# A fused attention and expert kernel: half-wide second-level products, paced transfers, and nine routing operations on GpSimd

## The chip, the cores and the metric

The kernel runs on one core of one Trainium2 chip. The time is device time in microseconds (us) of one launch, as the median of several runs. Engines are called as in the profile: PE is TensorE's matrix multiply, PEld its weight load, DVE is VectorE, ACT is ScalarE, POOL is GpSimd and SP is SyncE, which here only issues transfers.

## The reference: what is computed

```python
# attention: q, k, v of (8 batches, 8 heads, 576, 64), tau = 0.02
scores = np.matmul(q, k.transpose(0, 1, 3, 2)) / 8
thresh = np.max(scores, axis=-1, keepdims=True) - tau
scores = np.where(scores >= thresh, scores, -1e9)
attn = np.exp(scores - np.max(scores, axis=-1, keepdims=True))
attn = attn / (np.sum(attn, axis=-1, keepdims=True) + 1e-09)
x = np.matmul(attn, v).transpose(0, 2, 1, 3).reshape(4608, 512)
# experts: token_ids (4608,), w1 (8, 512, 1024), w2 (8, 1024, 512)
expert_idx = token_ids * 2654435761 % 8
for e in range(8):
    mask = expert_idx == e
    out[mask] = np.maximum(x[mask] @ w1[e], 0.0) @ w2[e]
```

Everything is fp32. Each of the 4608 rows of x goes through one expert, so about 576 rows fall to each.

## The kernel before, in words

**Attention (0 to about 466 us).** The work is cut into 32 pairs of heads, numbered p; head pair hp = p // 8 and batch b = p % 8. A pair has five steps: s = 0 takes the 64 last queries of both heads, s = 1 to 4 take 128 queries each. The main loop (L710 on) counts n = 5p + s up to LAST = 160 and a few steps more, and is written as one hand-made order of instructions, which the engines follow. In a step PE forms scores for the step after it (`score`, L235), DVE negates them with a running minimum (`negate`, L246), ACT takes the exponential (`expo`, L260), POOL computes the threshold (thr, L253), DVE masks (`mask`, L271), PE transposes the weights of the step before the last (L282), ACT copies them to SBUF (`put_wT`, L303), and PE multiplies them with v (L313). At s = 1 POOL adds the epsilon to the sums (`add_eps`, L343) and scales the next pair's keys (`scale_k`, L215); at s = 2 DVE takes the reciprocal (L740). At s = 0 of the pair after the next, DVE multiplies by it into the tile xm (`put_xm`, L352), and SP stores xm to x_scratch in DRAM, about 3.6 us until it has landed.

**Routing, beside attention.** `route()` is a Python generator whose pieces are put into the main loop at s = 3 and s = 0 (for p = 9, 11, 13 also at s = 2). It turns token ids into expert numbers, counts places per expert with a table of ones (`onehot`, 8 x 36 columns) and a running sum (`incl`), orders the experts by their row count (`key`, `pos`, `order`), and gives each token a slot (`base`, `rank`, `slot_i`). `scatters()` (L536 on) then writes the token numbers to their slots by 36 indirect transfers of POOL (L542), one at the end of a step except at s = 1, in pairs 13 to 21. `fetch_early` (L119, through `gather`) gathers 15 of the 20 column blocks of the first expert's x rows, head pairs 0 to 2, at the start of a step with s = 0 and at the end of one with s = 3 or 4, in pairs 26 to 31; the last five gathers follow attention.

**Experts (about 476 to 918 us).** Experts are worked on in order of their row count: e = 0 has 544 columns of rows, e = 1 to 4 have 576, e = 5 to 7 have 600 (layer 2 of e = 7: 480 and a remainder of 120, `last_tile`). Layer 1 is w1 (512 x 1024) in two groups of 256 + 256 output rows, layer 2 is w2 (1024 x 512). Layer 1 of e = 0 is done plainly (`early_h`, L640, and `late_h`, L658 to L666, which adds the last head pair's part). All others go through `seven`: a 2x2 block product with seven products of half-size blocks in place of eight (Strassen's scheme in Winograd's form: sums s1 to s4 of the left blocks, t1 to t4 of the right ones). Each product is 8 matmuls of 128 x 128 weights and of half the expert's columns (in layer 1, 4 in each of the two groups). DVE forms the sums of blocks (L858) and, from each product in PSUM, the running sums u2, u3, u4 and the outputs (L861), ACT copies the first product (p1, L951) and takes the relu (L948). The products take turns between two pairs of PSUM tiles (`bank2`).

Beside them, hung into the products as `side` work: DVE turns the next expert's gathered rows by 32x32 squares (`turn_x`, L1064) and SP moves them into xT; POOL gathers the rows of the expert after it (`fetch`); SP loads its weights; DVE transposes the outputs oT by squares (`put_squares`, L1033), and POOL sends each square of 32 rows to the output (L1042), with two copies of `stok_odd` after each as a pause (L1027).

Of the kernel before, what the change touches and what calls it, by code (L numbers as in the profile page):

```python
# [9 lines left out]
FP32 = mybir.dt.float32  # L10
# [10 lines left out]
def kernel(  # L21
# [122 lines left out]
    with tc.tile_pool(name="a_q", bufs=1) as a_q, \  # L144
# [221 lines left out]
        def route():  # L366
# [38 lines left out]
            nc.vector.tensor_copy(eidf[:], eid[:])  # L405
            yield
            yield
            nc.vector.tensor_tensor(out=onehot[:],
                                    in0=eidf[:, None, :].to_broadcast([P, E, NTC]),
                                    in1=iota_f[:, 0:E, None].to_broadcast([P, E, NTC]),  # L410
                                    op=ALU.is_equal)
            yield
            for e in (0, E // 2):
# [6 lines left out]
                if e == 0:  # L420
                    yield
            yield
            nc.vector.tensor_copy(row[:], incl[:, :, NTC - 1])
# [13 lines left out]
            nc.vector.scalar_tensor_tensor(out=key[:], in0=cnt[:, E:2 * E], scalar=float(E),  # L437
                                           in1=iota_f[:, 0:E], op0=ALU.mult, op1=ALU.add)
# [10 lines left out]
            for e0, d in STEPS:  # L449
# [15 lines left out]
            nc.vector.tensor_copy(ot[:], ot_i[:])  # L465
# [3 lines left out]
            nc.vector.tensor_tensor(out=base[:], in0=oend[:], in1=ot[:], op=ALU.subtract)  # L469
# [3 lines left out]
            nc.vector.scalar_tensor_tensor(out=base[:], in0=base[:], scalar=8192.0,  # L473
                                           in1=cnt[:, 0:E], op0=ALU.mult, op1=ALU.add)
            nc.gpsimd.tensor_tensor(out=base[:], in0=base[:], in1=pos[:], op=ALU.add)
            yield
            nc.vector.tensor_tensor(out=incl[:], in0=incl[:],
# [3 lines left out]
            nc.vector.tensor_tensor(out=incl[:], in0=incl[:], in1=onehot[:], op=ALU.mult)  # L481
# [189 lines left out]
        G0 = NS * ((HP - 1) * B + 2)  # L671
# [16 lines left out]
        with tc.manual_schedule():  # L688
# [21 lines left out]
            for n in range(LAST + NS + 1):  # L710
                p, s = divmod(n, NS)
                m = n - 2
                if s == 0:
                    fetch_early(n)
# [85 lines left out]
                if s != 1 and placed:  # L800
                    next(scatter_pieces, None)
                if s > 2:
                    fetch_early(n)
# [23 lines left out]
    with tc.tile_pool(name="m_x", bufs=1) as m_x, \  # L827
         tc.tile_pool(name="m_o", bufs=3) as m_o, \
# [9 lines left out]
        o_end = m_x.tile([P, DIN], FP32, name="o_end")  # L838
# [4 lines left out]
        w2_s = m_s.tile([P, 3, FH, D2], FP32, name="w2_s")  # L843
        h_s = m_s.tile([P, 3, FH, CH], FP32, name="h_s")
        halves = [m_s.tile([P, 2, CH], FP32, name=n) for n in ("p1", "u2", "u3", "u4")]
# [3 lines left out]
        turn = [0]  # L849

        def bank2():
            turn[0] ^= 1
            if turn[0]:
                return ps_sc.tile([P, 2, 512], FP32, name="sc")
            return ps_m.tile([P, 2, 512], FP32, name="bank2")
# [31 lines left out]
        def w2_sums(e):  # L887
            t = triple(w2_s, 0, FH)
            return t if e == E - 1 else [dealt(x, C2) for x in t]
# [19 lines left out]
        def sums_w2(e):  # L909
            s1 = None  # L910
            if e == E - 1:
                spare = w_pool.tile([P, CO, F], FP32, name="w1_sb")
                s1 = w_tiles["s1"] = spare[:, :, 0:D2]
            return left(*w2_blocks(e, w_tiles[e, 2]), w2_sums(e), s1)
# [11 lines left out]
        def seven(a, a_s, b, b_s, m0, outs, relu, after):  # L926

            (a11, a12, s1, a22), (s2, s3, s4) = a, a_s
            (b11, t1, b21, b22), (t2, t3, t4) = b, b_s
            c11, c12, c21, c22 = outs  # L930
            n_k, width, dealt_out = a11.shape[1], b11.shape[2], len(a11.shape) == 4
            p1, u2, u3, u4 = (t[:, :, 0:width] for t in halves)

            def product(x, y):
                ps = bank2()
                for i in range(2):
                    c0 = m0 + P * i
                    for c in range(n_k):
                        lhsT = (x[:, c, :, i] if dealt_out else
                                x[:, c, c0:c0 + P])  # L940
                        nc.tensor.matmul(ps[:, i, 0:width], lhsT=lhsT, rhs=y[:, c],  # L941
                                         start=c == 0, stop=c == n_k - 1)
                return ps[:, :, 0:width]

            def out(c, ps, u, step):
                add(c, ps, u)()
                if relu:
                    nc.scalar.activation(c, c, AF.Relu)  # L948
                after(step)

            nc.scalar.copy(p1, product(a11, b11))  # L951
            out(c11, product(a12, b21), p1, 0)
            add(u2, product(s2, t2), p1)()
            after(1)
            add(u3, product(s3, t3), u2)()
            after(2)
            out(c21, product(a22, t4), u3, 3)
            k5 = product(s1, t1)
            add(u4, k5, u2)()
            out(c22, k5, u3, 4)  # L960
            out(c12, product(s4, b22), u4, 5)

        def layer1(e, side):

            w, half = w_tiles.pop((e, 1)), caps[e] // 2
            for g in range(NG):
                outs = [h_0[:, FH * i + 2 * g:FH * i + 2 * g + 2, half * k:half * k + half]
                        for i in range(2) for k in range(2)]
                seven(w1_blocks(w), triple(w1_s, 0, C2), x_blocks(e), triple(x_s, 0, C2, half), 2 * P * g,
                      outs, True, lambda step: side(g, step))  # L970

        def layer2(e, side):
# [5 lines left out]
            if e == E - 1:  # L978
                a[2] = w_tiles["s1"]
            seven(a, w2_sums(e), h_blocks(0, FH, half),  # L980
                  triple(h_s, 0, FH, half), 0, outs, False, side)

        def last_tile(middle):

            w, o_sb, idx = w_tiles[E - 1, 2], o_end, gidx[:, KT - 1:KT]
# [11 lines left out]
        def put_out(e, *groups):  # L997
# [14 lines left out]
            for tr, kts in zip(trs, groups):  # L1012
                for i, kt in enumerate(kts):
                    rows = rows_of(kt)
                    o_sb = m_o.tile([P, DIN], FP32, name="o_sb")
# [8 lines left out]
        def pause():  # L1024

            for _ in range(2):
                nc.gpsimd.tensor_copy(stok_odd[:], stok[:])  # L1027
# [49 lines left out]
        with tc.manual_schedule():  # L1077
            run(sums_w2(0), 4)
            fill(18)
            late_h(lambda fo: (ps_sc.tile([P, 2, 512], FP32, name="sc") if fo in (2, 4) else  # L1080
                               ps_m.tile([P, 2, 512], FP32, name="bank2")))
            fetch(1)
            run(sums_h(0, 0, FH), 4)

        with tc.manual_schedule():
            for e in range(E):
# [3 lines left out]
                if e > 0:  # L1090
                    w2_work, h_work = sums_w2(e), sums_h(e, 0, 2)

                    def side1(g, step):
                        if g == 0:
                            run(w2_work)
                            if step == 0:
                                put_squares(e - 1, 1)
                        else:
                            run(h_work)
                        if step > 2:  # L1100
                            run(turns, 1 if g == 0 else 2)
# [3 lines left out]
                x_work = (sums_w1(e + 1) + sums_x(e + 1)) if more else []  # L1105

                def side2(step):
                    if step == 0:
                        run(turns, len(turns))
                    else:  # L1110
                        run(x_work, 2)
# [4 lines left out]
                    if more and step == 3:  # L1116
# [24 lines left out]
        with tc.For_i(0, n_ov, 1) as it:  # L1141
# [26 lines left out]
            o_sb = m_o.tile([P, DIN], FP32, name="o_sb")  # L1168
# [36 lines left out]
```

## Time and profile before

| what | value |
|---|---|
| median of 3 runs | 925.46 us (924.17 to 926.12) |
| the profiled execution | 926.27 us |
| its span, first to last instruction | 924.6 us |
| granted TensorE clock | 0.999 |
| PE / DVE / ACT / POOL busy | 906.9 / 759.9 / 457.3 / 550.1 us |
| attention's loop | 0 to about 466 us |
| experts' stage | about 476 to 918 us |
| last PE record ends | 917.7 us |

The profile is of one execution, 1.67 us longer than its span. A group of instructions shows the line, engine, operation, output and inputs with their shapes, the count, the busy time in us and the mean of one in ns, then the idle time before them. "[0.28 <-issue]" in the order of time means that the engine was idle for 0.28 us before the instruction and that no releaser is seen in the records. A wait is put down to the event that came last. Matmuls are pipelined, so their records overlap: two records' starts tell the rate, not their lengths.

### The profile page before, as it was taken

The page shows a single profiled execution, that of the slowest core. Times are in us where ns is not written, and L with a number is a line of the kernel's source. Part 1 is how long each engine was busy: PE and PEld are TensorE (multiplying, and loading weights), DVE is VectorE, ACT ScalarE, POOL GpSimd, SP SyncE. Part 2 cuts the span into 40 slices and gives each one's busy share as a digit, 9 for nine tenths or more (in the row PEclk, how much of TensorE's full clock was granted, in tenths as well). Part 3 has the DMA queues.
Part 4 walks back from the last instruction along what each step waited for, and adds up shares of the span by engine and source line. Part 5 has one row for each costly group of instructions (what it writes and reads, how often), then busy time and mean ns, then how long its engine had stood idle before and what let it go on. Part 6 is the DMA issues. An engine that isn't in the chain of part 4 may idle for free.

```text
span 924.6 us, 21039 instructions
## 1 busy us (share of the span) xinstructions
PE 906.9 (98%) x7495; PEld 661.6 (72%) x7495; DVE 759.9 (82%) x1654; ACT 457.3 (49%) x741; POOL 550.1 (59%) x842
## 2 busy tenths in 40 slices
PE   7999999999999999999999999999999999999997
PEld 4666666656666666565668879788887978879785
DVE  8999999999999999999945696867768685786741
ACT  6888888888888898788922020110202011020210
POOL 4233432456666623446414588787787877878773
PEclk9999999999999999999999999999999999999999
DMA  7454463554545668734011636445252543522001
GB/s 175 95 146 123 107 152 96 134 134 101 124 100 149 167 164 220 209 96 108 16 33 56 195 118 185 136 125 196 63 199 90 170 155 90 218 61 67 28 28 62
DMA packets 114777, 113.13 MB, mean 122 GB/s; under 512 B 32475, under 2 KB 89315, under 8 KB 114672
## 3 DMA queue, kind: packets, MB, share of 16 engines
q1 hardware_dynamic: 105168, 92.64, 37.0%
q0 software_dynamic: 9072, 18.91, 6.6%
q8 instruction: 61, 1.00, 0.4%
q14 instruction: 44, 0.36, 0.1%
q10 hardware_dynamic: 432, 0.21, 0.1%
HBM read 81.99 MB, written 21.44 MB: 112 GB/s over the span
## 4 chain that ended last, share of the span: by engine, by line
PE 83%; POOL 6%; issue 4%; DVE 3%; ACT 2%; DMA 1%; SPq 0%; POOLq 0%; DVEq 0%; ACTq 0%
PE bank L941 18%; PE av L313 18%; PE sc L941 18%; PE sc L235 14%; PE tr L282 11%; POOL out_dram L1042 4%; PE sc L640 3%; POOL stok_odd L1027 2%; PE av L282 1%; DVE ns L246 1%; DVE w L271 1%; ACT w L260 1%; DMA k_sb<-in_k_dram 1%; ACT wT_b L303 1%; PE bank L658 0%
## 5 line engine op out<-in xcount | busy, mean ns | idle before, releaser
L260 ACT ACTIVATE w<-ns,nmx 128x576 f32<-128x576 f32 x288 | 220.4, 776 | 28.6 <-DVE ns L246 27.9
L271 DVE SCALAR_TENSOR_TENSOR w<-ns,thr,w 128x576 f32<-128x576 f32 x288 | 225.7, 816 | 0.0
L253 POOL TENSOR_SCALAR thr<-nmx,drop 128x2 f32<-128x2 f32 (+1 forms) x160 | 104.4, 652 | 188.9 <-DVE ns L246 179.1
L246 DVE TENSOR_SCALAR_CACHE_REDUCE ns<-sc 128x576 f32<-128x576 f32 x288 | 205.7, 746 | 8.5 <-PE sc L235 7.7
L235 PE MATMUL sc<-k_sb,q 64*128 64x288 f32 (+1 forms) x1280 | 178.2, 422 | 1.1 <-DVE ns L246 0.6
L282 PEld LDWEIGHTS tr<-ident,w 64*128 64x128 f32 x2624 | 105.6, 138 | 96.9 <-ACT wT_b L303 35.3
L1042 POOL DMA_INDIRECT out_dram<-o_q,qidx x127 | 139.7, 1100 | 57.8 <-issue 49.2
L282 PE MATMUL tr<-ident,w 64*128 64x64 f32 x2624 | 139.2, 230 | 7.7 <-ACT wT_b L303 4.8
L1027 POOL COPY stok_odd<-stok 128x152 int32<-128x152 int32 x314 | 139.9, 445 | 10.0
L948 ACT ACTIVATE h<-h 128x576 f32<-128x576 f32 (+1 forms) x56 | 38.8, 693 | 142.8 <-DVE h L861 142.0
L235 PEld LDWEIGHTS sc<-k_sb,q 64*128 64x128 f32 (+1 forms) x1280 | 92.2, 177 | 23.5 <-DVE ns L246 9.8
L313 PE MATMUL av<-wT_a,v 128*64 128x320 f32 (+1 forms) x704 | 100.4, 418 | 0.2
L303 ACT COPY wT_a<-tr 128x512 f32<-128x512 f32 (+1 forms) x128 | 81.7, 638 | 20.6 <-PE tr L282 20.1
L303 ACT COPY wT_b<-tr 128x512 f32<-128x512 f32 (+1 forms) x128 | 81.3, 635 | 18.2 <-PE tr L282 10.2
L313 PE MATMUL av<-wT_b,v 128*64 128x256 f32 x640 | 83.2, 389 | 0.0
L313 PEld LDWEIGHTS av<-wT_a,v 128*64 128x64 f32 x704 | 43.7, 136 | 29.0 <-DVE xm L352 0.7
L951 ACT COPY p<-bank 128x576 f32<-128x576 f32 (+2 forms) x11 | 7.0, 634 | 107.5 <-PE bank L941 102.5
L313 PEld LDWEIGHTS av<-wT_b,v 128*64 128x64 f32 x640 | 40.2, 136 | 18.8 <-issue 0.7
L119 POOL DMA_INDIRECT xg<-x_scratch,gidx_x x35 | 41.8, 1193 | 19.2 <-issue 9.3
L542 POOL DMA_INDIRECT slot_scratch<-tok,slot_i x36 | 44.9, 1247 | 9.5 <-issue 7.6
L951 ACT COPY p<-sc 128x576 f32<-128x576 f32 (+2 forms) x11 | 7.0, 637 | 84.7 <-PE sc L941 79.8
L941 PE MATMUL bank<-h,w_sb 128*128 128x288 f32 (+3 forms) x192 | 48.1, 404 | 0.0
(198 smaller groups left out, 1402.4 us busy)
## 6 DMA issues: line engine op xcount, KB each, us to landing
w_sb<-in_moe_w_dram SPq DMA_DIRECT2D x16, 2048.0 KB
q<-in_q_dram SPq DMA_DIRECT2D x62, 288.0 KB
v<-in_v_dram SPq DMA_DIRECT2D x32, 256.0 KB
x_scratch<-xm SPq DMA_DIRECT2D x32, 256.0 KB
xT<-xq SPq DMA_DIRECT2D x84, 80.0 KB
k_sb<-in_k_dram SPq DMA_DIRECT2D x31, 144.0 KB
k_sb<-in_k_dram SPq DMA_DIRECT2D x32, 112.0 KB
x_scratch<-xg SPq DMA_DIRECT2D x9, 256.0 KB
```

Of the source, the lines that this page charges most:

```text
L235: nc.tensor.matmul(sc[out_rows, i, 0:S2], lhsT=q_sb[rows, h, q0:q1], rhs=k_sb[rows, h], start=True, stop=True)
L246: nc.vector.tensor_scalar(out=ns[:].rearrange("p (i s) -> p i s", i=2), in0=sc[:, :, 0:S2], scalar1=-1.0, scalar2=None, op0=ALU.mult, op1= ...
L253: nc.gpsimd.tensor_scalar(out=thr[:, 0:j + 1], in0=stats[n][0][:, 0:j + 1], scalar1=drop[:], scalar2=None, op0=ALU.add)
L260: nc.scalar.activation(w, nss[n, j][:], AF.Exp, bias=stats[n][0][:, j:j + 1], scale=-1.0)
L271: nc.vector.scalar_tensor_tensor(out=w, in0=nss.pop((n, j))[:], scalar=stats[n][1][:, j:j + 1], in1=w, op0=ALU.is_le, op1=ALU.mult, accum_ ...
L282: nc.tensor.transpose(dst[:, r, 64 * c:64 * c + 64], src[rows, c0:c0 + P], ident[rows, rows])
L303: nc.scalar.copy(dst, tr[:, :, 0:64 * n_c].rearrange("p r (c q) -> p r c q", c=n_c))
L313: nc.tensor.matmul(av[64 * j:64 * j + 64, g, c0:c1], lhsT=v_sb[:, c, 64 * j:64 * j + 64], rhs=wT[g][:, i, c0:c1], start=(c == 0), stop=stop)
L542: nc.gpsimd.indirect_dma_start(out=slot_dram[c % 2][:, :], out_offset=bass.IndirectOffsetOnAxis(ap=slot_i[:, c:c + 1], axis=0), in_=tok[:, ...
L941: nc.tensor.matmul(ps[:, i, 0:width], lhsT=lhsT, rhs=y[:, c], start=c == 0, stop=c == n_k - 1)
L1027: nc.gpsimd.tensor_copy(stok_odd[:], stok[:])
L1042: inst = nc.gpsimd.indirect_dma_start(out=rows[:, :], out_offset=bass.IndirectOffsetOnAxis(ap=idx, axis=0), in_=o_sb, in_offset=None, boun ...
```

## The change

Three things are changed.

1. **Routing.** Nine of the operations in `route()` go from DVE to POOL: the copies to eidf, row and ot, the one-hot table (one operation with two broadcast inputs becomes eight comparisons with a constant), the key (one operation becomes two), the two steps of base (the second becomes two), and the two large operations on incl. Their places between the yields stay nearly the same.
2. **Transfers.** Scatters stand at the end of steps s = 0 to 3 in place of 0, 2, 3 and 4. Early gathers begin one pair earlier and stand at the end of steps 2 and 3, and of step 4 only for n < 135; none stands at the start of s = 0. The last is at s = 2 of the last pair (n = 157).
3. **Experts.** `seven` is split into a class `Seven` whose methods can be interleaved, and whose products go on accumulating in a PSUM tile (start=False) in place of additions by DVE; ACT copies the partial results out. For e = 1 to 7 the product A12·B21 of either layer is done by a second level of the same scheme, class `Quarters`, for both groups of layer 1 at once: seven products of two matmuls each at half the width, in place of eight full matmuls. Four fixed PSUM tiles (`banks`) replace the turns. The sum s4 of w2 is written over A12 once ACT has copied A12's quarters away (`copy_quarters`). Some output tiles now use the x buffers, and a pause is one copy.

```diff
-            nc.vector.tensor_copy(eidf[:], eid[:])
-            yield
-            yield
-            nc.vector.tensor_tensor(out=onehot[:], in0=eidf[:, None, :].to_broadcast([P, E, NTC]),
-                                    in1=iota_f[:, 0:E, None].to_broadcast([P, E, NTC]), op=ALU.is_equal)
-            yield
+            nc.gpsimd.tensor_copy(eidf[:], eid[:])
+            for e0 in range(0, E, 3):
+                yield
+                for e in range(e0, min(e0 + 3, E)):
+                    nc.gpsimd.tensor_scalar(out=onehot[:, e], in0=eidf[:], scalar1=float(e),
+                                            scalar2=None, op0=ALU.is_equal)
...
-            nc.vector.scalar_tensor_tensor(out=key[:], in0=cnt[:, E:2 * E], scalar=float(E),
-                                           in1=iota_f[:, 0:E], op0=ALU.mult, op1=ALU.add)
+            nc.gpsimd.tensor_scalar(out=key[:], in0=cnt[:, E:2 * E], scalar1=float(E),
+                                    scalar2=None, op0=ALU.mult)
+            nc.gpsimd.tensor_tensor(out=key[:], in0=key[:], in1=iota_f[:, 0:E], op=ALU.add)
...
-            nc.vector.tensor_tensor(out=incl[:], in0=incl[:],
+            nc.gpsimd.tensor_tensor(out=incl[:], in0=incl[:],
                                     in1=base[:, :, None].to_broadcast([P, E, NTC]), op=ALU.add)
...
-            nc.vector.tensor_tensor(out=incl[:], in0=incl[:], in1=onehot[:], op=ALU.mult)
+            nc.gpsimd.tensor_tensor(out=incl[:], in0=incl[:], in1=onehot[:], op=ALU.mult)
...
-        G0 = NS * ((HP - 1) * B + 2)
+        G0 = NS * ((HP - 1) * B + 1)
...
-                if s == 0:
-                    fetch_early(n)
...
-                if s != 1 and placed:
+                if s < NS - 1 and placed:
                     next(scatter_pieces, None)
-                if s > 2:
+                if s in (2, 3) or s == 4 and n < G0 + 2 * NS:
                     fetch_early(n)
...
+        def products(ps, x, y, start, mid=None):
+            for i, lhsTs in enumerate(x):
+                for c, lhsT in enumerate(lhsTs):
+                    nc.tensor.matmul(ps[:, i], lhsT=lhsT, rhs=y[:, c], start=start and c == 0,
+                                     stop=c == len(lhsTs) - 1, skip_group_check=not start)
...
+        class Quarters:
...
+            def p1_p2(self):
+                products(self.x, self.a[0], self.b[0], True)
+                nc.scalar.copy(self.p1, self.x)
+                products(self.y, self.a[1], self.b[2], True)
+            def c11(self):
+                add(self.outs[0], self.y, self.p1)()
+            def p5_u2(self):
+                products(self.z, self.a[2], self.b[1], True)
+                nc.scalar.copy(self.p5, self.z)
+                products(self.x, self.a[4], self.b[4], False)
+                nc.scalar.copy(self.u2, self.x)
+            def c12_c22(self):
+                products(self.z, self.a[6], self.b[3], False)
+                add(self.outs[1], self.z, self.u2)()
+                products(self.x, self.a[5], self.b[5], False)
+                add(self.outs[3], self.x, self.p5)()
+            def c21(self):
+                products(self.x, self.a[3], self.b[6], False)
+                nc.scalar.copy(self.outs[2], self.x)
...
         def layer2(e, side):
...
+            o = Seven(a, w2_sums(e), h_blocks(0, FH, half), triple(h_s, 0, FH, half), 0, outs,
+                      False, *((banks[0], banks[1]) if e else (banks[3], banks[2])))
+            o.first()
+            o.keep_p1()
...
+            q = quarters_of(e, 2, *(banks[i][:, 0:1] for i in (2, 3, 3)))
+            q.p1_p2()
+            q.c11()
+            run(inner_b(second_blocks(e, 2)[1]), 4)
+            o.u2_sum()
+            q.p5_u2()
+            side(0)
+            o.u3_sum(True)
+            side(1)
+            q.c12_c22()
+            o.s1_t1(False)
+            side(2)
+            q.c21()
+            o.c11(o.p1)
+            o.c22(o.z)
+            o.c21()
+            side(3)
+            o.c12(lambda: side(4))
...
         def pause():
-            for _ in range(2):
-                nc.gpsimd.tensor_copy(stok_odd[:], stok[:])
+            nc.gpsimd.tensor_copy(stok_odd[:], stok[:])
...
-            run(sums_w2(0), 4)
+            w2_first = sums_w2(0)
+            run(w2_first, 3)
...
+            for _ in range(2):
+                banks += [ps_sc.tile([P, 2, 512], FP32, name="sc"),
+                          ps_m.tile([P, 2, 512], FP32, name="bank2")]
```

In layer 1 the quarters' products are interleaved with the first group's in the same way (`first`, `p1_p2`, `c11`, `u2_sum`, `p5_u2`, `s1_t1`, `c12_c22`, `u3_sum`, `c21`), and `side` work is dealt to eleven points by a table of counts. The squares of an expert's first half (`put_squares(e, 0)`) move from the fourth to the last side point of layer 2, for e = 0 to the start of the next layer 1.

## The prediction

> **What bounds the kernel now.** I read the page's totals first, then busy time by stretches of the span, then the DVE's waits, and last the order of time at the places that the change touches.
>
> ```profile
> span 924.6 us, 21039 instructions
> PE 906.9 (98%) x7495; PEld 661.6 (72%) x7495; DVE 759.9 (82%) x1654; ACT 457.3 (49%) x741; POOL 550.1 (59%) x842
> PE 83%; POOL 6%; issue 4%; DVE 3%; ACT 2%; DMA 1%; SPq 0%; POOLq 0%; DVEq 0%; ACTq 0%
> ```
> ```profile
> 200.00:300.00 100.00, 98.74 (x1219) 60.98 (x1216) 96.54 (x267) 85.98 (x140) 66.02 (x85) 1.00 0.50 121
> 530.00:700.00 170.00, 170.00 (x702) 144.08 (x701) 128.50 (x153) 22.96 (x35) 136.01 (x203) 1.00 0.48 152
> 700.00:900.00 200.00, 200.00 (x814) 166.67 (x813) 141.71 (x170) 28.31 (x42) 162.12 (x245) 1.00 0.32 97
> ```
> The columns are the stretch, then PE, PEld, DVE, ACT and POOL busy. From 530 on PE never stops at a granted clock of 1.00, so the experts' stage is PE's passes and nothing else. In attention (to 466 us) PE, DVE and ACT are all above 85 of 100: a ring in which each waits for the others a little. The two stages need separate sums.
>
> **Experts: passes.** Each fp32 matmul leaves two records, two passes.
>
> ```profile
> L941 PE MATMUL bank<-xT,w_sb 128*128 128x288 f32 x88 | 23.1, 406 | 0.0
> L941 PE MATMUL bank<-xT,w_sb 128*128 128x300 f32 x72 | 19.7, 416 | 0.0
> L941 PE MATMUL bank<-h,w_sb 128*128 128x240 f32 x16 | 3.4, 366 | 0.0
> ```
> The means, 406, 416 and 366 ns, hold pipeline overlap; what counts is start to start, and in the raw records that is 242.5, 252.5 and 202.5 ns at 288, 300 and 240 columns: columns/1.2 + 2.5. At half width that gives 122.5, 127.5 and 102.5. A layer's A12·B21 is 8 full matmuls (16 passes; layer 1's two groups together, layer 2's one); by the second level it is 14 of half width (28 passes).
> - 288 (e=1..4, two layers): 16×242.5 = 3.88 us becomes 28×122.5 = 3.43, −0.45, eight times: −3.60.
> - 300 (e=5, 6, and layer 1 of e=7): 4.04 becomes 3.57, −0.47, five times: −2.35.
> - 240 (layer 2 of e=7): 3.24 becomes 2.87, −0.37.
> Sum −6.32 us. The other six products keep their passes.
>
> **Does a half-wide pass wait for its weight load?** Each pass has a 128x128 load whose record is 190 ns, over 122.5. The nearest row is the last tile's product:
>
> ```profile
> 915.48 2.03 PEld L990 LDWEIGHTS sc<-w_sb,h 128*120 128x120 f32 x16
> 915.80 1.91 PE L990 MATMUL sc<-w_sb,h 128*120 128x128 f32 x16
> ```
> Sixteen passes of 128 columns run in 1.91 us with the last one's drain in it, 109 ns start to start (128/1.2 + 2.5), though each load's record is 183 ns: so the record is latency, not spacing. The Trainium skill (TensorE: Matmul & The Clock Gate, section LDWEIGHTS) puts a load at its columns over 1.2, 107 ns here. That speaks against the change only where a pass is shorter: 102.5 at e=7, 28×107 = 3.00, −0.24 in place of −0.37. If instead the 190 ns were the spacing, a product would cost 28×190 = 5.32 us, +1.44. I take row and rule.
>
> **Experts: adds and copies.** Sums that accumulate in PSUM take from DVE the additions for u2, u3 and u4 (L861, about 0.75 us each): 15.75 us per expert, against 6.75 + 2.25 of new additions and 6.4 of sums of quarters. DVE (about 36 of 50 us now) stays even. ACT gets copies at 0.634 us (the row of p, L951): from about 5.4 to 14 of 53 us, no bound. What counts is where PE now waits, since before it waited nowhere. No trace shows these waits.
> - *ACT's copy of p1 before the next accumulation*. The copy takes 0.634 + about 0.1 us of hand-over; the cover is one quarter product pair, 8×122.5 = 0.98 us, less the drain of the product that it reads (about 0.16+). Left is about 0.03; where it fails, up to 0.055 (a first pass without a prefetched load is 458 against 402 ns). Bounds 0 and 0.8 over 14 places: take +0.6.
> - *e=0's layer 2*. Its first product now goes to the bank that the last `late_h` product (fo=5) leaves; before, it took an older one:
>
> ```profile
> 500.72 1.08 PE L658 MATMUL bank<-xT,w_sb 128*128 128x272 f32 x4
> 501.63 3.90 PE L941 MATMUL sc<-h,w_sb 128*128 128x272 f32 x16
> 501.83 0.72 DVE L663 TENSOR_TENSOR h<-h,bank 128x544 f32<-128x544 f32 x1 [0.20 <-PE bank L658]
> ```
> The addition ends at 502.55; PE began at 501.63. So +0.9 (0.7 to 1.0).
> - *e=1's layer 1*. Its x lands late:
>
> ```profile
> 525.95 0.76 DVE L858 TENSOR_TENSOR x_s<-xT 128x576 f32<-128x576 f32 x1 [4.85 <-DMA xT<-xq]
> 526.74 0.76 DVE L858 TENSOR_TENSOR xT<-xT 128x576 f32<-128x576 f32 x1
> 527.42 2.02 DVE L1033 STREAM_TRANSPOSE o_q<-oT 128x1024 f32<-128x1024 f32 x1
> ```
> Behind 525.95 now stand four sums of x, four of quarters (0.33) and the 2.02 us transposition before the quarters' c11 addition, which frees a bank that PE wants about 1 us earlier. Also one 1.24 us sum goes before the turns of x. Between 0 and 2.5: take +1.2.
> - *layer boundaries*. The next layer 1's quarter product wants the bank that layer 2's c12 addition frees, queued behind ten sums (2×0.77, 4×0.45, 4×0.33 us) and a 2.27 us transposition. DVE gets there 27.7 to 28.4 us after the layer's start, PE 28.65 after it: slack 0.2 to 0.9, six times. Bounds 0 and 6 (1 us late each): take +1.0.
> - e=7's floor and single late loads: +0.3.
> Experts: −6.32 + 0.6 + 0.9 + 1.2 + 1.0 + 0.3 = **−2.3**. The squares' single pause (POOL about 1.75 in place of 2.1 us a square) is worth nothing: POOL's squares of e=6 end by 906, the last PE record is 917.7, and the 6.6 us from there to the end stay. The o_sb tiles that become x buffers were not waited for.
>
> **Attention: the transfers.**
>
> ```profile
> DVE ns L246 <- PE sc L235: 7.7, 25, 1.3
> DVE xm L352 <- issue: 2.5, 8, 0.6
> ```
> ```profile
> 402.73 1.37 POOL L119 DMA_INDIRECT xg<-x_scratch,gidx  x1 [0.16 <-issue]
> 403.13 0.76 DVE L246 TENSOR_SCALAR_CACHE_REDUCE ns<-sc 128x576 f32<-128x576 f32 x1
> 404.17 0.83 DVE L352 TENSOR_TENSOR xm<-av,rec 128x640 f32<-128x640 f32 x1 [0.28 <-issue]
> ```
> xm (first step of a pair) usually starts 0.68 us after its L246. Here it is 1.04, and xm begins as POOL's gather, issued at the end of the fifth step, ends (404.10). In nine pairs with such a transfer the delay is 0.3 to 0.7, 3.8 us in all; in five others with one there is none, so this is likely and not sure. The change has no scatter after the fifth step and only two gathers there, so most of it goes. A scatter now follows the second step, so its neighbour is the reciprocal (L740, of ten columns), not xm. Bounds 0 and −3.8; by the coincidence of ends I take −3.3. Gathers begin a pair earlier: the x rows that they read were stored at step 125, landing 3.6 us later, and the first gather is issued some 8 us after; the last one (step 157) has 8 us before its reader. Neither should wait.
>
> **Attention: nine operations.** DVE rows taken away: 183 + 451 + 158 + 160 + 161 + 167 + 161 + 450 + 452 = 2.34 us. But pairs that hold 0.45 us of them take 13.91 to 13.93 us against the 13.89 that undisturbed pairs take, in three of about eight cases: the ring has 0.45 us of room on DVE. What lies above the floor in the others (0.1 to 0.45) sums to −1.2. On POOL they cost one-hot 8×0.2, two large ones about 0.8 each (from 322 ns at 64 columns and 201 at 8: 2.2 ns a column), seven small at 0.2, about 4.6 us. POOL has 34 to 66 busy of 100, but it also makes thr for the masks: where routing made POOL late (178.1 us) a mask took 1310 in place of 812 ns. Bounds 0 and 1.5: take +0.5. The Trainium skill (GPSIMD Engine Reference, section 1, Specifications) says that GpSimd's SBUF interfaces are shared with VectorE and contend with instructions of two SBUF inputs; the mask is one. The rows: masks beside routing operations of POOL took 802, 808, 852 and 805 ns against 812 alone. By the rule up to 4.6 us would come back on DVE; by the rows nothing, and I follow them.
> Attention: −3.3 − 1.2 + 0.5 = **−4.0**.
>
> **Sum.** 926.27 (this execution; its span is 924.6) − 4.0 − 2.3 = 920.0. The median shown, 925.46, is 0.8 lower: **919.2**. Unexplained stalls in pairs 16, 21, 27 and 30 (1 to 2.3 us each) move by themselves with any change, so ±2 to 2.5 stands on this.
>
> **Rivals.**
> - *The experts' gain is eaten*: DVE is 0.5 us later than I count at each boundary and the copies of p1 always late: 6×0.5 more and so on, net 0. For it: PE has no slack and DVE is in order. Against: 0.2 to 0.9 slack. 926.27 − 4.0 − 0.8 = 921.5.
> - *Attention gives nothing*: the ring takes up DVE's room, and the delay of xm moves to whatever stands beside the scatter of the second step. For it: five pairs without delay. 926.27 − 2.3 − 0.8 = 923.2.
> - *No new wait at all*: −6.3 − 4.5 gives 914.7. Against: the e=0 wait follows from the bank.
> - *Slower: weight loads set the half-wide pass.* Place: 392 passes in 14 products. At the record's 190 ns the products cost +1.44 (288), +1.28 (300), +2.08 (240): +20.0, with −4.0 and the waits that remain about +2.5: about 944. It decides from 138.6 ns a pass, where 28 passes equal 16 of 242.5. For it: loads' records of 190, up to 308 ns in the strided w2. Against: 109 ns in the last tile.
>
> **How the numbers follow.** Chances: my sum 0.58 (own range 916.7 to 921.7), experts' gain eaten 0.14, attention nothing 0.12, no new wait 0.09, loads 0.07. A measurement tells about 0.2% from no change, 1.85 us. Faster by more: 0.58 + 0.13 + 0.06 + 0.09 = 0.86; within: 0.01 + 0.05 = 0.06; slower 0.08. The range 914.4 to 924.0 leaves out the loads and the ends of two other cases.
>
> **What would show it.** Right: matmuls of 144 columns 122.5 ns apart; an expert's period near 53.4 us where it was 54.3; PE waits at e=0's first layer-2 product (on DVE), at e=1's start and, small, on ACT's copies; xm's wait gone and pairs 13 to 31 nearer 13.89. Wrong: spacing near 190; boundary waits of 1 us or more; pair times as before; masks longer beside POOL's new rows.

## The result and the profile after

The changed kernel takes 920.35 us as a median of 6 runs (917.12 to 921.61), the kernel before 925.26 us (924.17 to 926.12, 6 runs). The ratio is 0.9943, with a 95% interval of 0.9929 to 0.9958: 4.9 us less. The prediction was 919.2, with a range of 914.4 to 924.0.

The profiled execution took 919.78 us, 6.49 less than the one of before. The page's totals, the chain of work that ended last, and busy time by stretches (PE, PEld, DVE, ACT, POOL):

```profile
span 918.1 us, 21471 instructions
...
PE 902.2 (98%) x7663; PEld 669.2 (73%) x7663; DVE 757.1 (82%) x1711; ACT 514.0 (56%) x848; POOL 500.6 (55%) x703
...
PE 48%; POOL 27%; issue 15%; DVE 3%; ACT 2%; SPq 1%; DMA 1%; POOLq 1%; DVEq 0%; ACTq 0%
```
```profile
200.00:300.00 100.00, 99.06 (x1232) 62.00 (x1228) 97.83 (x269) 86.75 (x142) 67.05 (x86) 1.00 0.53 127
...
530.00:700.00 170.00, 170.00 (x792) 148.62 (x791) 131.72 (x186) 51.18 (x85) 125.16 (x149) 1.00 0.48 152
...
700.00:900.00 200.00, 200.00 (x912) 172.61 (x911) 137.32 (x199) 54.36 (x94) 122.59 (x156) 1.00 0.31 96
```
ACT doubled in the experts' stage, as foreseen, and DVE stayed where it was. The chain that ended last now runs back through POOL's outputs (27%, 6% before), but POOL does not set the end: on that chain it does nothing from 884.96 to 903.45, and the stretch behind PE's last product takes 8.95 us for 8.83 before. PE still shows 170 of 170, but that no longer means full speed: records of waiting passes overlap too. So I measured by lengths. The first layer-2 product starts at 498.93 where it started at 501.63: attention and what follows it gave 2.70 us. From there to the start of the last product it is 410.25 where it was 414.17: the experts gave 3.92.

Expert by expert, the lengths are (e=0's layer 2 apart, 26.03 for 25.96):

| us | before | after | predicted by passes |
|---|---|---|---|
| layer 1 of e=1; of e=2 to 4 | 27.19; 27.16 | 26.84; 26.73 | −0.45 each |
| layer 2 of e=1 to 4 | 27.16 | 27.03 | −0.45 each |
| layer 1 of e=5 to 7 | 28.28 | 27.81 | −0.47 each |
| layer 2 of e=5, 6 | 28.28 | 28.09 | −0.47 each |
| layer 2 of e=7, to the last product | 29.50 | 29.49 | −0.37 |

Layer 1 gave 3.06 of 3.21 us, layer 2 only 0.93 of 3.11.

**Where layer 2 loses it.** This is PE in layer 2 of e=2, in order of time, with the ACT copy and the weight load that belong to one of the rows. A product of 16 passes takes 15 x 0.2425 + 0.406 = 4.04 us when nothing holds it.

```profile
605.55 4.04 PE L937 MATMUL sc<-h,w_sb 128*128 128x288 f32 x16
...
609.92 0.65 PE L937 MATMUL bank<-h,w_q 128*128 128x144 f32 x4
...
610.41 4.07 PE L937 MATMUL sc<-h_s,w_s 128*128 128x288 f32 x16
...
614.57 0.64 ACT L979 COPY u<-sc 128x576 f32<-128x576 f32 x1 [4.12 <-PE sc L937]
...
615.26 3.71 PEld L937 LDWEIGHTS sc<-h_s,w_s 128*128 128x128 f32 x16
...
615.29 4.12 PE L937 MATMUL sc<-h_s,w_s 128*128 128x288 f32 x16
...
620.23 4.15 PE L937 MATMUL bank<-h,w_sb 128*128 128x288 f32 x16
...
624.71 4.15 PE L937 MATMUL sc<-h_s,w_sb 128*128 128x288 f32 x16
...
628.70 4.04 PE L937 MATMUL bank<-h,w_sb 128*128 128x288 f32 x16
```
The half-width rows (0.65 for four: 3 x 0.1225 + 0.28) run as predicted. The full products behind them are long by 0.03, 0.08, 0.11 and 0.11 us, 0.33 in all; the two that follow a full product are 4.04. The view of waits names no wait of PE. The 0.08 is ACT's copy of u2: it ends at 615.21, and the load that waits for it starts at 615.26. The two of 0.11 have w_sb as weights, w2 itself with strided columns, and their load records are 308 ns, plain ones 190. In layer 1, whose weights are plain, no such row of e=2 to 7 is long by more than 0.02 us. (How far a strided load sticks out is measured below, under plain w2.)

**At 240 columns** the passes themselves are slower than columns/1.2 + 2.5. In layer 2 of e=7:

```profile
887.52 0.61 PE L937 MATMUL sc<-bi_s,wi_s 128*128 128x120 f32 x4
```
The raw starts in this row are 111.7 ns apart, not 102.5. The first narrow pass behind a wide one does take 102.5, as its load ran under the wide pass; so here it is the load that sets the spacing. The narrow passes lose 0.22 us by it and the copies take 0.12, so that nothing is left of the gain of 0.37.

**Attention's waits of DVE** and the order of time where the first of the early gathers stand:

```profile
DVE ns L246 <- PE sc L235: 6.1, 24, 0.8
...
DVE w L271 <- POOL thr L253: 4.2, 3, 2.6
```
```profile
361.54 0.44 SPq L358 DMA_DIRECT2D x_scratch<-xm  x1
...
363.69 0.72 POOL L253 TENSOR_SCALAR thr<-nmx,drop 128x2 f32<-128x2 f32 x1 [1.44 <-DVE ns L246]
...
368.36 1.13 POOL L119 DMA_INDIRECT xg<-x_scratch,gidx  x1 [3.94 <-DVE w L271]
...
369.53 0.31 POOL L253 TENSOR_SCALAR thr<-nmx,drop 128x2 f32<-128x2 f32 x1
...
369.88 0.82 DVE L271 SCALAR_TENSOR_TENSOR w<-ns,thr,w 128x576 f32<-128x576 f32 x1 [0.41 <-POOL thr L253]
```
```profile
383.56 1.10 POOL L119 DMA_INDIRECT xg<-x_scratch,gidx  x1 [4.82 <-DVE ns L246]
...
384.70 0.30 POOL L253 TENSOR_SCALAR thr<-nmx,drop 128x2 f32<-128x2 f32 x1
...
385.04 0.82 DVE L271 SCALAR_TENSOR_TENSOR w<-ns,thr,w 128x576 f32<-128x576 f32 x1 [1.24 <-POOL thr L253]
```
xm's wait of 2.5 us is gone from the list. A new one stands there: the mask waits for thr. POOL did nothing for 3.94 us in front of the gather. The row puts that down to DVE, but in the raw records POOL's queue comes to the gather at 363.79, right behind thr, and waits there 3.63 us, until the last of xm's three stores has landed (367.39). That store is late itself: SP issued it from 361.54 on, because the v load in front of it waited, to 360.86, for the semaphore of the 2 MB load of w1. At pair 26 no load holds up the store (issued from 378.17 on, landed at 382.62), and POOL waits for it all the same. thr stands behind the gather on POOL, and the mask behind thr.

From reciprocal to reciprocal (L738, L740 before), pairs 25 to 27 are 1.95 us longer than before; pairs 13 to 21 are 1.70 shorter, 1 to 12 0.60 shorter, 28 to 31 2.29. The 1.95 belong to this one execution: two later profiles of the same kernel, taken for the experiments below, name no wait of a mask for thr, and their pairs 25 to 27 take 43.2 and 42.9 us in all, where this one takes 46.1 and the profile of before 44.1.

### The profile page after: what moved, and what is told of

It is laid out like the page before. It is cut to its first block, busy times and chain, and to the rows that moved or that the text cites. A ratio compares the mean times of both kernels' runs of the same rounds, so it can differ in the third digit from the quotient of the medians.

```text
span 918.1 us, 21471 instructions
## 1 busy us (share of the span) xinstructions
PE 902.2 (98%) x7663; PEld 669.2 (73%) x7663; DVE 757.1 (82%) x1711; ACT 514.0 (56%) x848; POOL 500.6 (55%) x703
## 4 chain that ended last, share of the span: by engine, by line
PE 48%; POOL 27%; issue 15%; DVE 3%; ACT 2%; SPq 1%; DMA 1%; POOLq 1%; DVEq 0%; ACTq 0%
PE av L313 17%; POOL out_dram L1247 17%; PE sc L235 15%; PE tr L282 11%; POOL stok_odd L1232 8%; POOL xg L119 3%; PE sc L640 3%; PE av L282 2%; ACT w L260 1%; SPq L1277 1%; DVE w L271 1%; ACT wT_a L303 1%; DVE ns L246 1%; DMA k_sb<-in_k_dram 1%; POOLq L1247 0%
## 5 line engine op out<-in xcount | busy, mean ns | idle before, releaser
L246 DVE TENSOR_SCALAR_CACHE_REDUCE ns<-sc 128x576 f32<-128x576 f32 x288 | 205.3, 745 | 6.7 <-PE sc L235 6.1
L1247 POOL DMA_INDIRECT out_dram<-o_q,qidx x127 | 147.7, 1163 | 113.4 <-DVE o_q L1238 80.1
L253 POOL TENSOR_SCALAR thr<-nmx,drop 128x2 f32<-128x2 f32 (+1 forms) x160 | 100.7, 630 | 165.8 <-DVE ns L246 157.8
L1232 POOL COPY stok_odd<-stok 128x152 int32<-128x152 int32 x157 | 71.4, 455 | 0.6
L937 PE MATMUL bank<-h,w_sb 128*128 128x288 f32 (+4 forms) x248 | 62.0, 402 | 0.0
L937 PEld LDWEIGHTS bank<-h,w_sb 128*128 128x128 f32 x248 | 58.7, 290 | 0.5
L937 PE MATMUL sc<-h_s,w_s 128*128 128x288 f32 (+2 forms) x224 | 56.6, 406 | 0.0
L961 ACT ACTIVATE h<-h 128x576 f32<-128x576 f32 (+1 forms) x42 | 29.0, 692 | 41.4 <-DVE h L864 36.3
L119 POOL DMA_INDIRECT xg<-x_scratch,gidx_x x35 | 43.9, 1255 | 12.3 <-DVE xq L1269 5.3
```

Of the source, the lines that this page charges most:

```text
L119: nc.gpsimd.indirect_dma_start(out=dst, out_offset=None, in_=src, in_offset=bass.IndirectOffsetOnAxis(ap=idx, axis=0), bounds_check=src.sh ...
L246: nc.vector.tensor_scalar(out=ns[:].rearrange("p (i s) -> p i s", i=2), in0=sc[:, :, 0:S2], scalar1=-1.0, scalar2=None, op0=ALU.mult, op1= ...
L253: nc.gpsimd.tensor_scalar(out=thr[:, 0:j + 1], in0=stats[n][0][:, 0:j + 1], scalar1=drop[:], scalar2=None, op0=ALU.add)
L937: nc.tensor.matmul(ps[:, i], lhsT=lhsT, rhs=y[:, c], start=start and c == 0, stop=c == len(lhsTs) - 1, skip_group_check=not start)
L1247: inst = nc.gpsimd.indirect_dma_start(out=rows[:, :], out_offset=bass.IndirectOffsetOnAxis(ap=idx, axis=0), in_=o_sb, in_offset=None, boun ...
```

## Experiments

The runs come in three series (the recorded expectations say "call"), each on one chip beside the kernel before. The kernel before itself took 925.26 us in the first comparison and 918.20, 924.83 and 924.51 in the three series, so only differences within a series count.

| series | kernel | median, us (runs) | ratio to before, 95% |
|---|---|---|---|
| 1 (before 918.20) | experts only | 913.81 (5) | 0.9952 (0.9938 to 0.9966) |
| | attention only | 919.96 (15) | 1.0023 (1.0013 to 1.0033) |
| | loads early | 914.12 (5) | 0.9961 (0.9947 to 0.9974) |
| | gathers as before | 913.73 (5) | 0.9950 (0.9936 to 0.9964) |
| 2 (before 924.83) | the change | 918.39 (5) | 0.9929 (0.9916 to 0.9942) |
| | transfers only | 922.62 (7) | 0.9972 (0.9961 to 0.9984) |
| | routing only | 923.76 (21) | 0.9986 (0.9979 to 0.9994) |
| | plain w2 | 915.34 (4) | 0.9908 (0.9889 to 0.9927) |
| 3 (before 924.51) | the change | 916.58 (6) | 0.9927 (0.9910 to 0.9944) |
| | loads early | 917.12 (5) | 0.9917 (0.9904 to 0.9931) |
| | loads early, first blocks | 915.35 (4) | 0.9902 (0.9886 to 0.9917) |
| | second level in layer 1 alone | 926.76 (14) | 1.0026 (1.0015 to 1.0037) |

**Experts only.** The edit is the diff without its parts on `route()`, on the end of the steps and on G0.

> The kernel before with only the experts' part of the change. My reading of the two traces: the experts' stage is 3.9 us shorter (414.2 to 410.3 us from the first layer-2 product to the last product), in every run alike, so 925.3 - 3.9 = 921.4 us, with about the spread of before (2 us). Rival, that part of this gain came from attention's new order leaving DVE or POOL freer at the hand-over: the stage is then shorter by less than 3.5.

Measured −4.4 us, runs within 0.8 of each other (the 921.4 was for a kernel before at 925.3). The layers have the changed kernel's lengths to 0.04 us, with attention as before. So the experts' gain stands alone, and the rival fell.

**Attention only.** The rest of the diff.

> The kernel before with only routing and transfers changed. If the parts add up, what the medians leave beside the experts' 3.9 us is 1.0 us: 924.2 us, with single runs 3 to 4 us apart. The rival is the sum of my prediction, 4.0 us of gain: 921.3. In the trace I expect pairs 13 to 21 shorter by 1.7 us in all, and pairs 25 to 27 longer by about 2, where masks wait for a threshold behind a gather.

Measured: 1.8 us slower than before by the medians, runs 5.7 us apart where the kernel before has 1.6. No part of a gain is left. One reason lies in the kernel before: in this series its attention, which experts only has unchanged, has no late xm at all. Here is one of its 14 transfers beside an xm, to be set against 402.73 to 404.17 in the prediction:

```profile
397.06 1.37 POOL L119 DMA_INDIRECT xg<-x_scratch,gidx  x1 [0.16 <-issue]
...
397.46 0.76 DVE L246 TENSOR_SCALAR_CACHE_REDUCE ns<-sc 128x576 f32<-128x576 f32 x1
...
398.14 0.82 DVE L352 TENSOR_TENSOR xm<-av,rec 128x640 f32<-128x640 f32 x1
```
xm starts in the middle of the gather, 0.68 after its L246. Pairs 14 to 31 of that run stay within 0.2 us of 13.89 (the last one aside); in the profile of before, they were up to 2.3 longer. What the change takes away was not there to be taken. Of what it adds, the profile shows one piece: pair 27 takes 14.99 for 14.05, with a mask behind thr. That is 0.94 of the 1.8; the rest is not traced.

**Loads early.**

```diff
-                if s == 2 and p in (20, 24):
-                    load_w1(p // 4 - 5)
-                if s == 2 and p in (22, 26):
-                    load_w2((p - 22) // 4)
+                if s == 2 and p in (17, 21):
+                    load_w1((p - 17) // 4)
+                if s == 2 and p in (19, 23):
+                    load_w2((p - 19) // 4)
```

> The changed kernel with the four weight loads of attention moved from pairs 20, 22, 24 and 26 to 17, 19, 21 and 23, so that none is under way when gathers begin at pair 25. Theory: the store of xm is late because of the weight loads (behind one in SP's queue at pair 25, beside one on the transfer engines at pair 26), the gather waits for the store, the threshold behind the gather, and the mask for the threshold. Then the masks' wait for thr (4.2 us, three times) goes, and the time falls by about 2 us to 918.4, with less spread. Rival, that the ring takes these waits up or that gathers wait for any store: 920.3 and the masks' waits as they are.

914.12 us: the runs are 1.5 us apart in place of attention only's 5.7, and the time is the experts' alone (913.81) to 0.3. The masks' wait is gone from the list. POOL still waits for the store in front of the first gather, but thr comes in time behind it:

```profile
365.08 1.13 POOL L119 DMA_INDIRECT xg<-x_scratch,gidx  x1 [2.65 <-DVE ns L246]
```
The 1.5 us against the sum of the two parts (915.6) is not a direct comparison, since the changed kernel itself has no run in this series; that came in series 3:

> The changed kernel with the four weight loads of attention moved ahead of the gathers, now beside the changed kernel itself. Theory: masks no longer wait for a threshold behind a gather, -1.5 to -2 us against the changed kernel in either kind of call. Rival, that it was the call and not the loads: the same time as the changed kernel within 0.7 us.

There it gained nothing: 917.12 against 916.58, the rival's answer. In its profile one mask waits 0.8 us for thr, where the changed kernel's profile of the same series names no such wait:

```profile
369.44 1.13 POOL L119 DMA_INDIRECT xg<-x_scratch,gidx  x1 [4.32 <-DVE w L271]
...
370.97 0.82 DVE L271 SCALAR_TENSOR_TENSOR w<-ns,thr,w 128x576 f32<-128x576 f32 x1 [0.80 <-POOL thr L253]
```
POOL is done with the thr in front of this gather at 365.13, 0.6 us after the first of xm's three stores was issued (364.57); the last one lands at 368.37, 2.65 us after its own issue. So the gather is early even without a weight load, and that is what the runs show. That the loads make the masks' waits worse is not shown: these were 4.2, 0 and 0 us in three profiles of the changed kernel, 0 and 0.8 with the loads early. The runs of loads early are closer together in series 3 than the changed kernel's (1.6 us against 4.4), but in series 2 the latter were within 1.9 with the loads late.

**Gathers as before.** G0 and the places of `fetch_early` are taken back.

> The changed kernel with the 15 early gathers at their places of before (pairs 26 to 31, start of the first step and end of the fourth and fifth). Theory: the masks' waits of pairs 25 to 27 (about 2 us) go, and xm's delays beside gathers come back in pairs 28 to 30 (about 2 us): 920.3, same within 0.8. Rival, that the early gathers are a gain of their own: 922. Rival, that xm is not held by gathers at all: 918.4.

913.73. The three times were thought out for a kernel before near 925; the trace gives the third answer, with xm never late. Against the 915.6 that the two parts add up to, the early gathers were a loss in this series, though not by a direct comparison.

**The change again, in two series.**

> The changed kernel itself, beside the kernel before on one chip. In the last call the kernel before took 918.2 us where it had taken 925.3, and its xm was never late beside a scatter. If the parts add up on such a chip, the changed kernel takes -4.4 (experts) + 1.8 (attention) = -2.6 us against the kernel before, with runs 3 to 4 us apart. On a chip where the kernel before takes about 925, it is -4.9 again. Rival, that the first comparison holds on any chip: -4.9 at either.

> The changed kernel again, as the measure for the other runs of this call. Against the kernel before of the same call: -2.6 us if that takes about 918, -5 to -6.5 if it takes about 925; single runs 2 to 4 us apart.

−6.4 and −7.9 us by the medians (ratios 0.9929 and 0.9927), with the kernel before near 925. Both lie below the first comparison's 0.9943, and the intervals overlap with its own. The second is more than the −5 to −6.5 that I expected. The experts' stage, from the first layer-2 product to the last product, takes 410.4 us in both profiles (410.25 in the first), so what varies is attention: with 3.9 for the experts, the three medians leave it about 1.0, 2.5 and 4.0 us.

**Transfers only** and **routing only**, each with its part of the diff:

> The kernel before with only scatters and gathers moved. Theory: what attention's part loses is here, by masks behind a gather that waits for xm's store: +1.7 to +2.1 us against the kernel before and runs several us apart, where the kernel before takes 918; about -1.5 where it takes 925 and xm is late beside scatters. Rival, that GpSimd's new routing operations cost it: 0.

> The kernel before with only the nine routing operations on GpSimd. From the pair times of the last runs (pairs 1 to 13, -0.34 us in all): -0.3 us against the kernel before, on any chip; no masks slower than 820 ns beside GpSimd's new operations. My prediction's terms were -1.2 + 0.5 = -0.7. Rival, the shared SBUF interfaces: +1 or more.

Transfers: −2.2 us, a gain as expected of such a series. Routing: −1.1 (−1.9 to −0.6 by the interval), more than −0.3. With the experts' 3.9 that makes 7.2, where the changed kernel has 6.4 in this series. On POOL one and the same comparison of 36 columns took between 0.3 and 0.9 us, and the product with onehot 1.27. The masks beside the moved operations took 807 to 817 ns, the median of all masks being 811:

```profile
153.20 0.82 DVE L271 SCALAR_TENSOR_TENSOR w<-ns,thr,w 128x576 f32<-128x576 f32 x1
...
153.41 1.27 POOL L481 TENSOR_TENSOR incl<-incl,onehot 128x288 f32<-128x288 f32 x1
```

**Where a stall goes.** The changed kernel ran the same attention in series 2 as attention only did in series 1. First series 1, then series 2, the scatter at the end of the third step and ACT's next copy of 512 columns:

```profile
210.82 1.33 POOL L542 DMA_INDIRECT slot_scratch<-tok,slot_i  x1 [0.16 <-issue]
...
211.75 0.58 ACT L303 COPY wT_a<-tr 128x512 f32<-128x512 f32 x1
```
```profile
209.70 1.33 POOL L542 DMA_INDIRECT slot_scratch<-tok,slot_i  x1 [0.16 <-issue]
...
211.08 0.58 ACT L303 COPY wT_a<-tr 128x512 f32<-128x512 f32 x1 [0.40 <-PE tr L282]
```
In series 2 the copy begins 0.05 us after the scatter's end, 0.40 us after ACT could take it; in series 1 it begins inside the scatter. Six such copies, each beginning where a scatter ends, are 0.23 to 0.41 us late in series 2, and none is in series 1. It is the picture of xm before, on another engine: a pair with it takes 14.25 to 14.37 where 13.89 is the floor, as five of pairs 14 to 21 do. Pairs 13 to 21 stand 1.9 us above that floor in all, where the profile of before has 3.8. So with the scatters moved, the delay sits at ACT's copy in place of DVE's xm, and half of it came back.

**Plain w2.** `w2_blocks` takes plain columns for every expert, so that the output's columns come in another order.

```diff
-            return [dealt(w[:, FH * j:FH * j + FH], CO)[:, :, :, C2 * i:C2 * i + C2]
-                    for i in range(2) for j in range(2)]
+            return [w[:, FH * j:FH * j + FH, D2 * i:D2 * i + D2]
+                    for i in range(2) for j in range(2)]
```

> The changed kernel with w2's blocks taken as plain columns for every expert, as it does for the last one; the output's columns then come in another order, the work is the same. Theory: the first full-width pass after a half-width one waits 0.11 us in layer 2 because its strided weight load has a record of 308 ns, 118 more than a plain one, and 122.5 ns of cover. With plain loads two of four gaps go: layer 2 of e=1 to 6 takes 26.8 in place of 27.03 us (27.85 in place of 28.08 at 300 columns), -1.3 us in all against the changed kernel. Rival, that the gaps come with any change of width: 27.03 as before.

Layer 2 took 26.80 us and 27.87. The two products with w_sb are back at 4.04:

```profile
611.73 4.12 PE L934 MATMUL sc<-h_s,w_s 128*128 128x288 f32 x16
...
616.66 4.04 PE L934 MATMUL bank<-h,w_sb 128*128 128x288 f32 x16
...
621.03 4.04 PE L934 MATMUL sc<-h_s,w_sb 128*128 128x288 f32 x16
```
The stride is the cause of the two gaps of 0.11; the one behind ACT's copy (4.12) stays. What a strided load costs by itself can be seen in layer 2 of e=0, which has no narrow pass. Its first product, in the changed kernel and with plain w2:

```profile
498.93 3.90 PE L937 MATMUL bank<-h,w_sb 128*128 128x272 f32 x16
```
```profile
495.60 3.83 PE L934 MATMUL bank<-h,w_sb 128*128 128x272 f32 x16
```
In the raw records most passes of 272 columns start 233 to 234 ns apart with strided weights, and 229.2 with plain ones (columns/1.2 + 2.5). So strided loads follow each other at about 233.5 ns. Behind a pass of 242.5 that is hidden; behind one of 122.5 it leaves 111 ns, which is the gap. At 300 columns it leaves 233.5 − 127.5 = 106, and 102 is measured. The same pace makes e=0's layer 2 0.07 us longer than before: s4 of w2 now lies in w2's own tile, so that five of its seven products have these weights in place of four.

The median is 3.1 us below the changed kernel's, of which the experts' stage accounts for 1.5, with 1.4 of that in layer 2 of e=1 to 6.

**First blocks.** On top of loads early, in `layer2`:

```diff
             q.p5_u2()
+            if e < E - 1:
+                for i in (2, 3):
+                    nc.scalar.copy(w2_q[:, i - 2, 0], a[i][:, 0, :, 0])
+                    o.a[i][0][0] = w2_q[:, i - 2, 0]
```

> As the last, and in layer 2 of e=1 to 6 ACT copies the first 128x128 weight block of the two strided products that follow half-width ones into plain tiles that are free by then; the other blocks stay strided. Theory: only the first load after a half-width pass sticks out, so layer 2 takes 26.8 in place of 27.03 us (27.86 in place of 28.08) as with plain columns everywhere, -1.3 us more. Rival, that the second strided load is late as well: half of that or nothing.

Layer 2 took 26.81 and 27.88 us: one plain block in front is enough. The product's first two passes and the other fourteen:

```profile
616.64 0.65 PE L937 MATMUL bank<-h,w_q 128*128 128x288 f32 x2
...
617.12 3.56 PE L937 MATMUL bank<-h,w_sb 128*128 128x288 f32 x14
```
915.35 us, 1.8 below loads early in the same series and 1.2 below the changed kernel: the fastest kernel of that series, and its runs do not overlap with those of the other two.

**Second level in layer 1 alone.**

```diff
-            q.p1_p2()
-            q.c11()
-            run(inner_b(second_blocks(e, 2)[1]), 4)
+            o.second(banks[2])
             o.u2_sum()
-            q.p5_u2()
             side(0)
             o.u3_sum(True)
...
```
The rest of the edit, cut here, takes the quarters' later products, their sums and the copies of A12 out of layer 2 as well, and gives s4 of w2 a tile of its own.

> The changed kernel with the second level in layer 1 alone; layer 2 does A12 times B21 by eight full matmuls, still accumulating in PSUM. Theory from the layers' lengths: layer 2's second level is worth 0.13 us a layer at 288 columns, 0.19 at 300 and nothing at 240, so +0.9 us against the changed kernel, layer 2 at 27.16 or a little more. Rival, the pass count alone as in my prediction: +3.1 us.

926.76 us, 10.2 above the changed kernel: neither answer. The experts' stage alone is 8.2 longer (418.6 for 410.4). Layer 2 takes 28.22 us, and the waits of PE name the reason:

```profile
PE sc L936 <- ACT u L978: 5.4, 7, 0.8
```
```profile
618.40 4.16 PE L936 MATMUL sc<-h_s,w_s 128*128 128x288 f32 x16 [0.78 <-ACT u L978]
```
The product for u3 goes on in the bank that ACT is still copying u2 out of. In the changed kernel the quarters' four matmuls lie between the two. Start to start the gap is 1.06 us a layer (0.95 and a late load of 0.11), and 28.22 − 1.06 = 27.16, what layer 2 took before the change. So my experiment also took away a cover, seven times, and what it measured is this: in layer 2 the second level is worth 0.13 us by its passes, and 1.06 as the work that hides ACT's copy, in this order of products.

## Why the prediction held, point by point

**The sum held, its parts less.** Predicted −4.0 for attention and −2.3 for the experts; the profiled pair shows −2.7 and −3.9. Two errors of opposite sign nearly cancel, and to that extent the closeness of 919.2 to 920.35 is luck. It also belongs to the first comparison alone: the experts' 3.9 stands in every profile of the change, attention's share does not.

**Passes.** 122.5 and 127.5 ns held. At 120 columns a pass takes 111.7 ns, above both columns/1.2 + 2.5 (102.5) and the 107 estimated from the Trainium skill's columns over 1.2 for a load of 128 columns (TensorE: Matmul & The Clock Gate, section LDWEIGHTS). The slower rival, loads at their record's 190 ns, fell; a form of it is real, for the first pass behind a half-width one when the load is strided. An expert's period is 53.8 us, where 53.4 was to show me right and 54.3 was before.

**New waits of PE: 4.0 predicted, 2.4 measured.**
- The bank of e=0's first layer-2 product, +0.9 predicted, 0 measured. PE goes on at 498.93, ahead of the addition that I thought it waits for:

```profile
498.93 3.90 PE L937 MATMUL bank<-h,w_sb 128*128 128x272 f32 x16
...
499.13 0.72 DVE L663 TENSOR_TENSOR h<-h,bank 128x544 f32<-128x544 f32 x1 [0.20 <-PE bank L658]
```
So that bank cannot be the one that the addition still reads; which tile was in it I did not follow further. What e=0's layer 2 lost is the 0.07 us of its strided s4.
- e=1's start, +1.2 predicted, 0.13 measured, in two places: 0.07 behind ACT's copy of p1 (it ends at 527.79, the load that waits for it starts at 527.84), and 0.06 behind the addition that frees the bank (530.77 and 530.82).
- Layer boundaries, +1.0 predicted, none measured: the slack of 0.2 to 0.9 us held six times.
- ACT's copies, +0.6 predicted, 0.7 measured, but almost only in layer 2 (0.05 us in layer 1 of e=2 to 4), and mostly at u2's copy, not p1's.
- "Single late loads" and e=7, +0.3 predicted: 1.3 for the twelve strided loads and 0.22 for e=7's passes. This is the term that was too small. I saw the 308 ns in the trace and asked whether they limit full passes, not what lies in front of the first one.

**Transfers: −3.3 predicted; in the profiled pair −1.7 in pairs 13 to 21, −2.3 in pairs 28 to 31 and 2 us given back in pairs 25 to 27.** xm's wait went as said. Two steps failed. "The first gather is issued some 8 us after": POOL's queue comes to it 2.2 us after the store's first issue (363.79 and 361.54), because it reaches it right behind thr, in the middle of the step, and not at its end. What that costs differs: the masks' wait for thr was 4.2 us in one profile of the changed kernel and 0 in two. And in my sum I asked where the stall goes only on DVE; it went to ACT, as the rival "whatever stands beside the scatter" had left open.

**Routing: −0.7 predicted, −1.1 (−1.9 to −0.6) measured**, and the masks were not slowed (807 to 817 ns). POOL paid instead: 9.3 us for the moved operations where I had 4.6.

**The rival that attention gives nothing came true in one series** (1.8 us slower, before at 918.20), for a reason that I hadn't given: the delay of xm, 3.8 us of it in the profile of before, is in some series and not in others. What decides that stays open. The chip alone does not: the record names the same chip, number 14, for series 1 and 2. The traces show only that the delayed instruction starts where POOL's transfer ends, that the same instructions lie beside the same transfers undelayed in another series, and that 6.6 us of the kernel before go with it.

## What to carry to other kernels

A narrower pass has to hide the same weight load: look at the first full pass behind a narrow one, and at strided weights first; one plain block there was worth as much in these layers as plain weights everywhere. An indirect transfer that waits in a queue takes with it everything queued behind it, so count from when the queue reaches it, and follow the store that it waits for back through the queue that issues it. When a product is left out, ask what its time was hiding. And read a second profile of the same kernel before a wait is called its cost: the masks' wait of 4.2 us stood in one of three.

## What the runs showed of the hardware that I had not expected

- Passes of 120 columns with plain 128x128 fp32 weights start 111.7 ns apart, but 102.5 where the load ran under a wide pass: plain loads follow each other at 111.7 ns, with records of 190.
- Loads of strided weights (record 308 ns) follow each other at about 233.5 ns. They cost nothing behind passes of 242.5 ns, some 4 ns a pass at 272 columns, and 0.11 us behind a pass of 122.5.
- The kernel before took 918.2 us in one series and 924.5 to 925.3 in the three others, with no instruction changed. Its attention in experts only (series 1), set against the profile of before, differs in the pairs with scatters and gathers.
